# First feed-forward of a fused attention and two feed-forwards: six blocks of 512 tokens for eight of 384, and three weight slots shared by two tiles each

## The chip, the cores and the metric

One core of one Trainium2 chip runs the whole program. The metric is device time in microseconds; the kernel before takes 1082.54 us, the median of three runs (1082.47 to 1082.88).

## The reference

```python
# attention: 4 batch rows, 8 heads, 768 tokens, 64 wide; chunks of 32 tokens
# a chunk sees 16 tokens to its left, 8 to its right and 8 memory tokens
scores = (q_c @ k_full.transpose) / 8
a = softmax(scores); out[chunk] = a @ v_full
x = out as [3072 tokens, 512]
# first feed-forward: 512 -> 2048 -> 512
h = x @ w_in
g = where(h > 0, h, exp(min(h, 0)) - 1)
x = g @ w_out
# second feed-forward: 512 -> 1024 -> 1024 -> 512
a = x @ w1; b = x @ w2
out = ((a * b) @ w3) @ w_out2
```

The weights of both feed-forwards arrive as 64-bit floats and are decoded on the chip.

## The kernel before

Every value of a product is held as two tiles, a high part (`fp32r`) and a low part (the rest), and every product is three matmuls: high by high, high by low, low by high (`mm3`, L125 to L127 for the first feed-forward and the product of weights, L690 to L692 in `mm_half` for the second).

**Tiling.** Attention works on groups of 128 tokens (four chunks); 24 groups G, six to a batch row. The first feed-forward works on blocks of `TB` = 384 tokens, so three groups (`GPB`) make the input of a block, `xhl[j % 2]`. A block has 16 chunks f of 128 hidden features. For chunk n (counted over all blocks) `mm_h(n)` makes 12 matmuls into one of two PSUM banks, `elu_exp`, `elu_max`, `elu_hi`, `elu_lo` make g of it on ScalarE and VectorE, and `mm_x(n - 2)` makes 12 matmuls from an earlier chunk's g into four PSUM banks that gather over the block. `store_x1` writes a finished block to DRAM. The 32 weight tiles (16 of `w_in`, 16 of `w_out`) lie in slots `W[0]` to `W[31]`.

**Order of work.** The order on each engine is the one in which the code is written. Before the first matmul of block 0 stands `START`, a list of attention steps for the groups 0, 1, 2 (u and t: transposes of `head`, q and k; s: scores; m: max and exp; z, n, p: sums, normalising, 32x32 flip into `pT`; v: values; o: output split into `xhl`; k and w: loads) and steps f of the weight decoder `feed`. Groups 1 and 2 have PSUM pairs of their own; all other groups use `banks` (`PA`).

The attention of the later groups runs among the matmuls. Each chunk has two half-steps, called `at_step`: one behind `mm_h`, one behind `mm_x`. `base(G)` gives a group's first half-step, `paces["slow"]` the place of each of its steps behind that, with 32/3 half-steps from group to group. The same table places the decoding of the second feed-forward's weights: `wos` and `w3s` (a `w3` tile is turned by four TensorE transposes into `banks`, L442, and split into `st` by L173 and L176), and `duos` (differences of w1 and w2). At most two `st` tiles are live; a store to DRAM frees one.

In block 0 the decoder still works on `w_in` and `w_out`: per job a load of 512 KB, `rebase` (L160), `top` (L182) and a cast (L173) on ScalarE, `merge` (L186) or `shift` and `low` (L164, L168), and a split (L176) on VectorE.

Behind the blocks `mm_wc` multiplies the two last weight matrices (512 columns), and the second feed-forward takes four pairs of 384-token halves by seven products in place of eight.

Of the kernel before, what the change touches and what calls it, by code (L numbers as in the profile page):

```python
# [20 lines left out]
def tile_kernel(  # L21
# [24 lines left out]
    P = 128  # L46
# [13 lines left out]
    TB = 384  # L60
    NB = NT // TB
    GPB = TB // GQ
# [21 lines left out]
    W = [None if i in LATER else const.tile([P, 2, 512], F32R, name=f"w{i}") for i in range(2 * FF1)]  # L84
# [4 lines left out]
    PB = [pb_p.tile([P, 2, 512], F32, name=f"pair{i}") for i in range(GPB - 1)]  # L89
# [4 lines left out]
    x1d = [dram.tile([P, KT, TB], F32, name=f"x1d{j}") for j in range(NB)]  # L94

# [102 lines left out]
    class Feed:  # L198
# [19 lines left out]
        def step(self):  # L218
# [30 lines left out]
    def at_tile(G, pool, shape, name, tag=None):  # L249
        tag = tag or name  # L250
        if 0 < G < GPB:
            pool, tag = early_p, f"{tag}{G}"
        return pool.tile(shape, F32, tag=tag, name=name, bufs=1)
# [10 lines left out]
    def banks(G):  # L264
        return PB[G - 1] if 0 < G < GPB else PA

# [8 lines left out]
    def load_qk(G):  # L275
# [5 lines left out]
        kn_g = k_t[G] = at_tile(G, qk_p, [P, H, D], "kn") if 0 < G < GPB else kn  # L281
# [8 lines left out]
    def load_v(G):  # L290
# [5 lines left out]
        vw_g = v_t[G] = at_tile(G, v_p, [P, 2, H, D], "vw") if 0 < G < GPB else vw  # L296
        nc.sync.dma_start(out=vw_g[p0:P, 0], in_=by_token(v, b, t0 + p0, t0 + P))
        for c in range(NCG):
# [3 lines left out]
            if g == 0 or G < GPB:  # L302
# [187 lines left out]
    def store_next():  # L490
# [17 lines left out]
    def base(G):  # L508
        return 2 * FF1 * (G - GPB) // GPB + 1, "slow"
# [11 lines left out]
    def plan_duo(s0, duo):  # L521
        plan(s0, duo.jobs[0], (-1, rebase), (0.1, shift), (0.2, mid_low))
        plan(s0, duo.jobs[1], (1, rebase), (1.3, shift), (2.3, mid_low))
# [8 lines left out]
    DUOS = (1, 2, 4, 7, 10, 11, 13, 16)  # L532
    for G in range(GPB, NG):
        s0, pace = base(G)
        for at, fn in zip(paces[pace], chain):
# [3 lines left out]
        if G - GM in DUOS:  # L539
            plan_duo(s0, duos.pop(0))  # L540
        elif wos:
            plan(s0, wos.pop(0), (2, rebase), (3.5, shift), (4.5, mid_low), (5.1, mid_hi), (6.1, mid_lo))
        if w3s and G - GM not in (2, 11):
            plan(s0, w3s.pop(0), (5, rebase), (6.2, shift), (7.6, mid_low), (9.1, mid_flip), (9.6, mid_flip_lo))
# [106 lines left out]
    NPAIR = NB // 2  # L651
# [10 lines left out]
    def load_x1(p):  # L662
        for r in range(2):
            for k in range(2):
                t = late.tile([P, 2, TB], F32, tag=f"x1{r}{k}", name="x1")
                nc.sync.dma_start(out=t, in_=x1d[2 * p + r][:, 2 * k:2 * k + 2, :])
                x1_t[p, r, k] = t

    def left_step(p, i):
        a11, a12, a21, a22 = (x1_t[p, r, k] for r in range(2) for k in range(2))  # L670
        if i == 3:
            x1_t[p, "s1"] = sub(late.tile([P, 2, TB], F32, tag="s1", name="s1"), a21, a22, ALU.add)
        s1 = x1_t.get((p, "s1"))
        if i == 4:
            sub(a21, a11, a21)
            sub(a11, s1, a11)
        if i == 6:
            sub(a12, a12, a11)
        src = (a11, a12, a22, s1, a11, a21, a12)[i]
# [16 lines left out]

    def mm_step(n, last, between, stored):

        y, z = PS[4][:, 0:TB], PS[5][:, 0:TB]
# [15 lines left out]
        nc.scalar.copy(r1, y)  # L715
        mm_half(n, z, "a12", "b21", True, True)
        sub(c11, z, r1, ALU.add)
        do(0)
        mm_half(n, y, "s2", "t2", False, True)
        nc.scalar.copy(r2, y)  # L720
        do(1)
        mm_half(n, z, "s1", "t1", True, True)
        nc.scalar.copy(r5, z)
        do(2)
        mm_half(n, y, "s3", "t3", False, True)
        sub(c22, y, r5, ALU.add)
        do(3)
        mm_half(n, z, "s4", "b22", False, True)
        sub(c12, z, r2, ALU.add)
# [3 lines left out]
        sub(c22, y, c22, ALU.mult)  # L733
# [218 lines left out]
```

## Time and profile before

| | |
|---|---|
| median of three runs | 1082.54 us |
| profiled execution | 1081.98 us |
| its span, first to last instruction | 1080.2 us |
| TensorE matmul busy | 1044.0 us (97%) |
| VectorE busy | 573.2 us (53%) |
| ScalarE busy | 468.6 us (43%) |
| start, up to the first matmul of block 0 | 36.8 us |
| block 0 | 85.0 us |
| blocks 1 to 6 | 468.7 us |
| block 7 | 68.6 us |
| product of weights | 45.3 us |
| second feed-forward | 375.8 us |

A block is counted from its first matmul out of `xhl` to that of the next. Matmuls are pipelined and their ends are modelled, so the time that one matmul costs is read from start to start, not from its duration.

### The profile page before, as it was taken

The page shows a single profiled execution, that of the slowest core. Times are in us where ns is not written, and L with a number is a line of the kernel's source. Part 1 is how long each engine was busy: PE and PEld are TensorE (multiplying, and loading weights), DVE is VectorE, ACT ScalarE, POOL GpSimd, SP SyncE. Part 2 cuts the span into 40 slices and gives each one's busy share as a digit, 9 for nine tenths or more (in the row PEclk, how much of TensorE's full clock was granted, in tenths as well). Part 3 has the DMA queues.
Part 4 walks back from the last instruction along what each step waited for, and adds up shares of the span by engine and source line. Part 5 has one row for each costly group of instructions (what it writes and reads, how often), then busy time and mean ns, then how long its engine had stood idle before and what let it go on. Part 6 is the DMA issues. An engine that isn't in the chain of part 4 may idle for free.

```text
span 1080.2 us, 20847 instructions
## 1 busy us (share of the span) xinstructions
PE 1044.0 (97%) x8528; PEld 987.5 (91%) x8528; DVE 573.2 (53%) x1061; ACT 468.6 (43%) x984; POOL 1.7 (0%) x16
## 2 busy tenths in 40 slices
PE   4799999999999999999999999999999999999998
PEld 3788999999999999999999998799999999999997
DVE  4899667566565566566564334143443544443323
ACT  3788555555455555555554442032232222222222
POOL 0000000000000000000000000000000000000000
PEclk9999999999999999999999999999999999999999
DMA  8967356455455456454351865354565565555521
GB/s 192 292 177 212 107 174 184 132 166 155 131 161 174 143 158 183 147 169 142 100 163 44 296 215 172 131 181 143 172 217 208 169 217 208 171 167 188 182 78 59
DMA packets 170090, 180.40 MB, mean 167 GB/s; under 512 B 101388, under 2 KB 140300, under 8 KB 169996
## 3 DMA queue, kind: packets, MB, share of 16 engines
q1 hardware_dynamic: 168956, 178.81, 53.7%
q8 instruction: 67, 1.10, 0.4%
q10 hardware_dynamic: 1040, 0.26, 0.1%
q14 instruction: 27, 0.22, 0.1%
HBM read 139.20 MB, written 39.85 MB: 166 GB/s over the span
## 4 chain that ended last, share of the span: by engine, by line
PE 86%; DVE 6%; ACT 5%; issue 1%; DMA 1%; SPq 0%; ACTq 0%; DVEq 0%
PE bank L125 18%; PE bank L126 18%; PE bank L127 18%; PE bank L691 7%; PE bank L692 7%; PE bank L690 7%; PE banks L407 2%; PE banks L127 2%; PE banks L126 2%; PE banks L125 2%; PE banks L348 1%; PE banks L324 1%; DVE w L176 1%; DVE eg L574 1%; PE banks L326 1%
## 5 line engine op out<-in xcount | busy, mean ns | idle before, releaser
L125 PE MATMUL bank<-xhl,w 128*128 128x384 f32 x512 | 176.3, 344 | 0.7 <-ACT xhl L121 0.7
L125 PE MATMUL bank<-g,w 128*128 128x384 f32 x512 | 175.2, 342 | 0.0
L126 PE MATMUL bank<-g,w 128*128 128x384 f32 x512 | 171.4, 335 | 1.1 <-DVE g L582 1.1
L126 PE MATMUL bank<-xhl,w 128*128 128x384 f32 x512 | 171.9, 336 | 0.0
L127 PE MATMUL bank<-xhl,w 128*128 128x384 f32 x512 | 171.9, 336 | 0.0
L127 PE MATMUL bank<-g,w 128*128 128x384 f32 x512 | 171.3, 335 | 0.0
L578 ACT CAST g<-eg 128x384 fp32r<-128x384 f32 x128 | 66.0, 516 | 98.4 <-DVE eg L574 98.0
L574 DVE SCALAR_TENSOR_TENSOR eg<-eg,bank 128x384 f32<-128x384 f32 x128 | 70.2, 548 | 59.6 <-ACT eg L569 59.6
L125 PEld LDWEIGHTS bank<-xhl,w 128*128 128x128 f32 x512 | 96.6, 189 | 3.6 <-ACT xhl L121 0.9
L568 ACT ACTIVATE eg<-bank 128x384 f32<-128x384 f32 x128 | 62.8, 490 | 84.0 <-PE bank L127 83.9
L474 DVE TENSOR_TENSOR e<-bank,e 128x384 f32<-128x384 f32 x64 | 35.7, 558 | 118.9 <-PE bank L692 72.8
L126 PEld LDWEIGHTS bank<-g,w 128*128 128x128 f32 x512 | 96.2, 188 | 1.8 <-DVE g L582 1.8
L125 PEld LDWEIGHTS bank<-g,w 128*128 128x128 f32 x512 | 96.1, 188 | 1.1
L126 PEld LDWEIGHTS bank<-xhl,w 128*128 128x128 f32 x512 | 96.7, 189 | 0.4 <-DVE xhl L122 0.4
L127 PEld LDWEIGHTS bank<-xhl,w 128*128 128x128 f32 x512 | 96.5, 189 | 0.0
L127 PEld LDWEIGHTS bank<-g,w 128*128 128x128 f32 x512 | 96.1, 188 | 0.0
L738 ACT CAST g<-e 128x384 fp32r<-128x384 f32 x64 | 29.7, 512 | 145.9 <-DVE e L474 145.9
L582 DVE TENSOR_TENSOR g<-eg,g 128x384 fp32r<-128x384 f32 x128 | 70.6, 552 | 18.3 <-ACT g L578 18.3
L691 PE MATMUL bank<-xd,w 128*128 128x384 f32 x224 | 75.8, 338 | 0.0
L692 PE MATMUL bank<-xd,w 128*128 128x384 f32 x224 | 75.6, 337 | 0.0
L690 PE MATMUL bank<-xd,w 128*128 128x384 f32 x224 | 74.9, 334 | 0.0
L569 ACT ACTIVATE eg<-eg 128x384 f32<-128x384 f32 x128 | 67.3, 526 | 4.1
(145 smaller groups left out, 1829.6 us busy)
## 6 DMA issues: line engine op xcount, KB each, us to landing
w<-wqd SPq DMA_DIRECT2D x96, 512.0 KB
raw<-in_moe_w_dram SPq DMA_DIRECT2D x32, 512.0 KB
wqd<-st SPq DMA_DIRECT2D x24, 512.0 KB
raw<-in_moe_w_out_dram SPq DMA_DIRECT2D x20, 512.0 KB
w3d<-st SPq DMA_DIRECT2D x16, 512.0 KB
w<-w3d SPq DMA_DIRECT2D x16, 512.0 KB
w<-wqd SPq DMA_DIRECT2D x32, 256.0 KB
raw<-in_moe_w_in_dram SPq DMA_DIRECT2D x12, 512.0 KB
```

The costliest lines, as they stand in the source:

```text
L125: mm(o, lhsT=w_hi, rhs=x_hi, start=start, stop=False)
L126: mm(o, lhsT=w_hi, rhs=x_lo, start=False, stop=False)
L127: mm(o, lhsT=w_lo, rhs=x_hi, start=False, stop=stop)
L474: nc.vector.tensor_tensor(out=o, in0=a, in1=b, op=op)
L568: nc.scalar.activation(e, h_t[n], AF.Relu, scale=-1.0)
L569: nc.scalar.activation(e, e, AF.Exp, scale=-1.0)
L574: nc.vector.scalar_tensor_tensor(out=e, in0=e, scalar=-1.0, in1=h_t.pop(n), op0=ALU.add, op1=ALU.max)
L578: nc.scalar.copy(g_t[n][:, 0, :], eg_t[n])
L582: nc.vector.tensor_tensor(out=g[:, 1, :], in0=eg_t.pop(n), in1=g[:, 0, :].bitcast(F32), op=ALU.subtract)
L690: mm(o, lhsT=args[0], rhs=args[2], start=start and i == 0, stop=False, skip_group_check=more)
L691: mm(o, lhsT=args[0], rhs=args[3], start=False, stop=False, skip_group_check=more)
L692: mm(o, lhsT=args[1], rhs=args[2], start=False, stop=i == 1, skip_group_check=more)
```

## The change

The first feed-forward takes blocks of 512 tokens, so four groups make a block, there are six blocks, and a matmul has 512 columns. The second feed-forward keeps 384 (`TP`, `GPP`); it fetches its input from the 512-token blocks in up to two pieces.

`START` makes group 3 as well, with the q and k tiles, PSUM banks and `vw` of group 0, and has six decoder steps for five. The number of early PSUM pairs stays at two (`EARLY`).

The larger tiles need room. Slots 2, 3 and 4 hold the `w_out` tiles 24, 25 and 26 too: both are saved to DRAM (`shd`) after they were decoded, and in each block the slot is loaded with the one when the other was read (`fill`). The spare load buffers of the decoder fall from four to two; two tiles of the second feed-forward lie in other tiles' free columns, and `s1` is made in place.

A group gets 8 half-steps, with one pace for all. The `w3` turn moves from the half-step 9 of a group to 5, the values from 8 to 7, the output to 7.2, the first transposes of a batch row (`at_first`) to -0.5. Each odd group takes a `duo` and a `w3` tile, each even one a `wo` and a `w3` tile.

```diff
-    TB = 384
+    TB, TP = 512, 384
     NB = NT // TB
-    GPB = TB // GQ
+    GPB, GPP = TB // GQ, TP // GQ
+    EARLY = 3
...
-    RAWS, SPARE, SPARE_JOBS = 4, 4, 16
-    LATER = (10, 11, 12, 13, 14, 15, 25, 26, 27, 28, 29, 30, 31)
-    START = "u0 t0 f s0 t1 f m0 s1 z0 n0 m1 p0 t2 v0 s2 z1 n1 p1 m2 o0 k3 w3 v1 z2 n2 p2 f o1 v2 f o2 f"
+    RAWS, SPARE, SPARE_JOBS = 4, 2, 16
+    LATER = (11, 12, 13, 14, 15, 27, 28, 29, 30, 31)
+    SHARED = {2: 24, 3: 25, 4: 26}
+    START = "u0 t0 k3 f s0 t1 f m0 s1 z0 n0 m1 p0 t2 v0 w3 s2 z1 n1 p1 m2 o0 t3 v1 s3 z2 n2 p2 f o1 v2 m3 f o2 z3 n3 p3 k4 v3 w4 f o3 f"
...
+    for i, j in SHARED.items():
+        W[j] = W[i]
...
+            if 0 <= i - 3 < len(self.jobs) and self.jobs[i - 3].slot in shd:
+                slot = self.jobs[i - 3].slot
+                nc.sync.dma_start(out=shd[slot], in_=W[slot].bitcast(F32))
...
     def banks(G):
-        return PB[G - 1] if 0 < G < GPB else PA
+        return PB[G - 1] if 0 < G < EARLY else PA
...
-    paces = {
-        "slow": (-1, 0, 0, 2, 3, 4, 5, 6, 8, 8, 9), "fast": (-0.5, 0, 0, 1, 1.5, 2, 2.5, 3, 4, 4, 4.5),
-        "mid": (-1, 0, 0, 2, 3, 4, 5, 5, 7, 7, 7.5),
-    }
+    pace = (-0.5, 0, 0, 2, 3, 4, 5, 6, 7, 7.2, 7.5)
...
     def base(G):
-        return 2 * FF1 * (G - GPB) // GPB + 1, "slow"
+        return 2 * FF1 * (G - GPB) // GPB
...
-            (4.5, lambda d: d.hi(3, d.block(1, 1))), (5.1, Duo.lo),
-            (6.8, duo_first), (6.9, lambda d: d.hi(1)), (7.5, Duo.lo),
-            (10.3, duo_second), (10.4, lambda d: d.hi(2)), (11.1, Duo.lo),
+            (3.2, lambda d: d.hi(3, d.block(1, 1))), (4.2, Duo.lo),
+            (7.5, duo_first), (7.6, lambda d: d.hi(1)), (8.1, Duo.lo),
+            (8.2, duo_second), (8.3, lambda d: d.hi(2)), (9.1, Duo.lo),
...
+    def plan_w3(s0, at):
+        plan(s0, w3s.pop(0), (at, rebase), (max(at + 0.7, 3.6), shift), (4.2, mid_low), (5.1, mid_flip), (6.1, mid_flip_lo))
...
+            for a, b in SHARED.items():
+                if 1 <= j < NB and f == a + 1:
+                    fill(b, shd[b])
+                if j < NB - 1 and f == b - FF1 + 3:
+                    fill(a, shd[a])
```

Three places show how the order moves. In the changed kernel L122 has become L128, L176 is L182, L186 is L192, L317 is L326, L328 is L337, L365 and L366 are L374 and L375, L407 is L416, and L568 and L569 are L582 and L583.

VectorE at the start, behind the flip of group 2 (out of `e_538` before, `e_586` now); `pair_100`, `pair_101` and `banks` are the PSUM of the groups 1, 2 and 0 or 3. Before:

```order
L186 SCALAR_TENSOR_TENSOR f<-f,raw 128x512
L122 TENSOR_TENSOR xhl_73<-pair_100,xhl_73 128x2x4x64
L176 TENSOR_TENSOR w_75<-f,w_75 128x512
L186 SCALAR_TENSOR_TENSOR f<-f,raw 128x512
L122 TENSOR_TENSOR xhl_73<-pair_101,xhl_73 128x2x4x64
L176 TENSOR_TENSOR w_76<-f,w_76 128x512
L186 SCALAR_TENSOR_TENSOR f<-f,raw 128x512
L176 TENSOR_TENSOR w_77<-f,w_77 128x512
```

Now, with the passes of group 3 (L374, L375 and L382 on) between the output splits and the weights:

```order
L192 SCALAR_TENSOR_TENSOR f<-f,raw 128x512
L128 TENSOR_TENSOR xhl_73<-pair_100,xhl_73 128x2x4x64
L374 TENSOR_REDUCE mx<-banks 128x8
L375 TENSOR_TENSOR e<-banks,mx 128x512
L182 TENSOR_TENSOR w_75<-f,w_75 128x512
L192 SCALAR_TENSOR_TENSOR f<-f,raw 128x512
L128 TENSOR_TENSOR xhl_73<-pair_101,xhl_73 128x2x4x64
L382 TENSOR_REDUCE sm<-e 128x8
L383 TENSOR_SCALAR sm<-sm 128x8
L384 RECIPROCAL sm<-sm 128x8
L385 TENSOR_TENSOR rc<-sm,odd 128x16
L394 TENSOR_TENSOR e_653<-e,rc 128x16x32 x2
```

Group 3's max and subtract moved in ahead of the first weight's split, its sums and normalising ahead of the second's.

ScalarE in chunk 0 of block 0: the exponent of that chunk (`eg`, out of `bank_95`) and the copies of the first interleaved group's q and k (`qT`, `kT`). Before, the exponent comes first:

```order
L568 ACTIVATE eg<-bank_95 128x384
L569 ACTIVATE eg<-eg 128x384
L173 CAST w_78<-f 128x512
L160 ACTIVATE f<-more 128x512
L328 COPY qT<-banks 128x512
L331 COPY kT<-banks 128x16x32
L332 COPY kT<-banks 128x4x3x24
L333 COPY kT<-front 128x4x24
```

Now the six copies stand ahead of it:

```order
L179 CAST w_78<-f 128x512
L166 ACTIVATE f<-raw 128x512
L337 COPY qT<-banks 128x512
L340 COPY kT<-banks 128x16x32
L341 COPY kT<-banks 128x4x3x24
L342 COPY kT<-front 128x4x24
L343 COPY kT<-memo 128x16x8
L345 COPY front<-banks 128x96
L582 ACTIVATE eg<-bank_95 128x512
L583 ACTIVATE eg<-eg 128x512
```

The copies moved from behind the exponent and two decoder passes of the next weight to ahead of it, since the group's transposes stand one half-step earlier.

TensorE where a batch row ends (block 0, group 5 and the `head` of group 6): `pT,vw` are the values. Before, two sets of 12 matmuls lie between the values and the `head` transposes:

```order
L127 MATMUL bank_96<-xhl_73,w_1113 128x384
L407 MATMUL banks<-pT,vw 64x64 x32
L125 MATMUL bank_606<-g,w_1118 128x384
...
L127 MATMUL bank_609<-g,w_1119 128x384
L317 MATMUL banks<-ident,head 128x16 x4
L125 MATMUL bank_95<-xhl_74,w_75 128x384
```

Now nothing lies between them, and the next chunk's matmuls stand behind:

```order
L132 MATMUL bank_724<-g,w_91 128x512
L133 MATMUL bank_724<-g,w_91 128x512
L416 MATMUL banks<-pT,vw 64x64 x32
L326 MATMUL banks<-ident,head 128x16 x4
L131 MATMUL bank_95<-xhl_73,w_83 128x512
L132 MATMUL bank_95<-xhl_73,w_83 128x512
```

The `head` transposes moved up to the values of the group before, which use the same banks.

## Rows read from the trace of the kernel before

**Rows 1.** Page, part 1: engine, busy us (share of the span) x instructions.

```profile
PE 1044.0 (97%) x8528; PEld 987.5 (91%) x8528; DVE 573.2 (53%) x1061; ACT 468.6 (43%) x984; POOL 1.7 (0%) x16
```

**Rows 2.** Windows: from:to length, busy us of each engine, clock, DMA share, GB/s.

```profile
36.80:121.80 85.00, 78.08 (x785) 73.99 (x785) 74.53 (x136) 70.11 (x143) 0.00 (x0) 1.00 0.68 187
121.80:590.50 468.70, 466.54 (x4826) 451.24 (x4825) 287.53 (x566) 248.35 (x544) 0.00 (x0) 1.00 0.50 149
```

**Rows 3.** Timeline of TensorE, last block: start us, us, what; ends are modelled.

```profile
590.50 0.33 PE L125 MATMUL bank<-xhl,w 128*128 128x384 f32 x1
...
659.14 0.39 PE L125 MATMUL bank<-w,w 128*128 128x512 f32 x1
```

**Rows 4.** Timeline, weight product, 512 columns: first and last of 26 matmuls.

```profile
661.90 0.39 PE L125 MATMUL bank<-w,w 128*128 128x512 f32 x1
...
667.57 0.39 PE L126 MATMUL bank<-w,w 128*128 128x512 f32 x1
```

**Rows 5.** Timeline, all engines, start of the program; [idle before <-what ended it].

```profile
17.23 1.11 PE L324 MATMUL pair<-ident,qn 128*128 128x128 f32 x4
...
22.45 0.57 ACT L328 COPY qT<-pair 128x512 f32<-128x512 f32 x1
...
24.06 0.26 ACT L336 COPY front<-pair 128x96 f32<-128x96 f32 x1
...
25.29 1.25 SPq L141 DMA_DIRECT2D more<-in_moe_w_in_dram  x1
...
26.70 0.65 DVE L365 TENSOR_REDUCE mx<-pair 128x8 f32<-128x512 f32 x1
...
29.34 0.69 DVE L122 TENSOR_TENSOR xhl<-banks,xhl 128x512 fp32r<-128x512 f32 x1 [1.25 <-ACT xhl L121]
...
32.63 1.25 DVE L396 STREAM_TRANSPOSE pT<-e 128x1024 f32<-128x1024 f32 x1
...
33.80 0.65 DVE L186 SCALAR_TENSOR_TENSOR f<-f,raw 128x512 int32<-128x512 int32 x1
...
33.94 2.22 PE L407 MATMUL pair<-pT,vw 64*64 64x64 f32 x64 [4.88 <-DVE pT L396]
...
34.37 0.68 DVE L122 TENSOR_TENSOR xhl<-pair,xhl 128x512 fp32r<-128x512 f32 x1
...
34.48 0.62 ACT L173 CAST w<-f 128x512 fp32r<-128x512 f32 x1 [3.08 <-DVE f L186]
...
36.20 0.59 ACT L121 CAST xhl<-pair 128x512 fp32r<-128x512 f32 x1
...
36.83 0.69 PE L125 MATMUL bank<-xhl,w 128*128 128x384 f32 x1 [0.68 <-ACT xhl L121]
```

**Rows 6.** Timeline of TensorE, first block.

```profile
38.05 0.52 PE L127 MATMUL bank<-xhl,w 128*128 128x384 f32 x1
...
40.29 0.50 PE L125 MATMUL bank<-xhl,w 128*128 128x384 f32 x1
...
61.88 1.28 PE L407 MATMUL banks<-pT,vw 64*64 64x64 f32 x64 [1.84 <-DVE pT L396]
```

**Rows 7.** Timeline, values and output split of one group, sixth block.

```profile
455.07 1.16 PE L407 MATMUL banks<-pT,vw 64*64 64x64 f32 x64
...
456.16 0.45 PE L125 MATMUL bank<-xhl,w 128*128 128x384 f32 x1
...
456.94 0.69 DVE L122 TENSOR_TENSOR xhl<-banks,xhl 128x512 fp32r<-128x512 f32 x1 [2.82 <-ACT xhl L121]
```

**Rows 8.** Timeline of TensorE, fourth block: weight flip; wait ahead of the q transposes.

```profile
302.10 0.60 PE L442 MATMUL banks<-ident,f 128*128 128x128 f32 x4
302.45 0.42 PE L125 MATMUL bank<-g,w 128*128 128x384 f32 x1
...
304.45 0.34 PE L127 MATMUL bank<-g,w 128*128 128x384 f32 x1
305.15 0.65 PE L324 MATMUL banks<-ident,qn 128*128 128x128 f32 x4 [0.36 <-DVE st L176]
```

More of the change, by code (lines that the diff above doesn't have):

```diff
@@ L88, in tile_kernel @@
     pb_p = early_psum.enter_context(tc.tile_pool(name="pb_p", bufs=1, space=PSUM))
-    PB = [pb_p.tile([P, 2, 512], F32, name=f"pair{i}") for i in range(GPB - 1)]
+    PB = [pb_p.tile([P, 2, 512], F32, name=f"pair{i}") for i in range(EARLY - 1)]
     w3d = [[dram.tile([P, 2, 512], F32, name=f"w3d{h}_{c}") for c in range(FF2)] for h in range(2)]
@@ L94, in tile_kernel @@
     x1d = [dram.tile([P, KT, TB], F32, name=f"x1d{j}") for j in range(NB)]
+    shd = {i: dram.tile([P, 2, 512], F32, name=f"shd{i}") for pair in SHARED.items() for i in pair}
     early_ctx, w_ctx = ExitStack(), ctx.enter_context(ExitStack())
@@ L538, in tile_kernel @@
             continue
-        if G - GM in DUOS:
+        if G % 2:
             plan_duo(s0, duos.pop(0))
[L541 to L544, printed above, removed]
+            plan_w3(s0, 2.6)
+        elif G % GPB:
+            plan_wo(s0, 1)
+            plan_w3(s0, 2.6)
+        else:
+            plan_w3(s0, 3.4)
+            plan_wo(s0, 5.1)
     assert not wos and not w3s and not duos, (len(wos), len(w3s), len(duos))
@@ L732, in mm_step @@
         do(5)
-        sub(c22, y, c22, ALU.mult)
+        sub(c22, cut(y), c22, ALU.mult)
         sub(c11, c11, c12, ALU.mult)
@@ L805, in tile_kernel @@
                 late = ctx.enter_context(tc.tile_pool(name="late", bufs=1, side="right"))
-                more = [late.tile([P, 2, 2, TB], F32R, name=f"xc{i}") for i in range(3)]
+                more = [late.tile([P, 2, 2, TP], F32R, name=f"xc{i}") for i in range(3)]
                 left.append({})
                 for i, what in enumerate(LEFTS[:4]):
-                    left[0][what] = [xhl[i // 2][:, r, i % 2 * 2:i % 2 * 2 + 2, :] for r in range(2)]
+                    left[0][what] = [xhl[i // 2][:, r, i % 2 * 2:i % 2 * 2 + 2, 0:TP] for r in range(2)]
                 for i, what in enumerate(LEFTS[4:]):
@@ L860, in tile_kernel @@
             if n >= NH - FF1:
-                free = [f] if n < NH else []
+                free = [f] if n < NH and f not in SHARED else []
                 if n >= NH - FF1 + 2:
@@ L898, in tile_kernel @@
         end = ctx.enter_context(tc.tile_pool(name="end", bufs=1))
-        more = [end.tile([P, 2, 2, TB], F32R, name=f"xd{i}") for i in range(len(LEFTS))]
-        left.append({what: [t[:, r] for r in range(2)] for what, t in zip(LEFTS, more)})
-        e_f.update(enumerate([eg_p.tile([P, TB], F32, tag="eg", name="eg") for _ in range(2)] + [end.tile([P, TB], F32, name=f"e{i}") for i in range(4)]))
-        gq.extend([g_p.tile([P, 2, TB], F32R, tag="g", name="g") for _ in range(3)] + [end.tile([P, 2, TB], F32R, name="g3")])
+        gs = [g_p.tile([P, 2, TB], F32R, tag="g", name="g")[:, :, 0:TP] for _ in range(3)]
+        more = [end.tile([P, 2, 2, TP], F32R, name=f"xd{i}") for i in range(len(LEFTS) - 1)]
+        more = [[t[:, r] for r in range(2)] for t in more] + [[gs.pop(), end.tile([P, 2, TP], F32R, name="xd")]]
+        left.append(dict(zip(LEFTS, more)))
+        es = [eg_p.tile([P, TB], F32, tag="eg", name="eg")[:, 0:TP] for _ in range(2)]
+        es += [end.tile([P, TP], F32, name=f"e{i}") for i in range(4)]
+        e_f.update(enumerate(cut(e) for e in es))
+        gq.extend([[cut(g[:, i, :]) for i in range(2)] for g in gs])
+        gq.extend([[x[:, i, 0:GPP, TP:TB] for i in range(2)] for x in xhl])
         NA = NPAIR * FF2
@@ L915, in stored @@
                     store_out(p - 1, t)
-            mm_step(n, n == NA, {t: lambda t=t: behind(t) for t in range(2 * GPB)}, stored)
+            mm_step(n, n == NA, {t: lambda t=t: behind(t) for t in range(2 * GPP)}, stored)
             if n < NA:
```

68 lines of the change are left out of this document (38 added, 30 removed).

## The prediction

> **What bounds the kernel now.** I read the page's busy shares first: TensorE is busy for 97% of the span [rows 1]. So a change is worth what it takes off TensorE's own stream, or what it adds to the time in which TensorE waits. I then cut the span at the stage borders [rows 2]. The first block of the first feed-forward lasts 85.0 us, of which TensorE is busy for 78.1; in the same stretch VectorE is busy for 74.5 and ScalarE for 70.1, because the weights are decoded there. The next six blocks last 468.7 us with TensorE idle for only 2.2. The last block has no attention in it and the stages behind it are full as well. Outside the first 122 us the matmul stream therefore sets the pace.
>
> In the stream I took the distance from start to start, since the busy time of one matmul (0.33 us) overlaps with the next. The last block is 396 matmuls of 384 columns in 659.14 - 590.50 = 68.64 us, 173.3 ns each [rows 3]. The same three-term product with 512 columns stands in the stage that multiplies the two weight matrices: 25 matmuls in 667.57 - 661.90 = 5.67 us, 226.8 ns each [rows 4]. The difference is 53.5 ns for 128 columns; at 2.4 GHz 128 columns take 53.3. So each matmul has a fixed 13 ns that doesn't depend on its columns, and that is what the wider block saves.
>
> **The change, part by part.**
>
> *Wider matmuls.* 3072 matmuls of 384 columns become 2304 of 512, the same columns. 3072 x 173.3 = 532.4 us become 2304 x 226.8 = 522.5 us: **-9.9 us**, all of it on the path. The bound on the good side is this value. On the other side, the first twelve 512-column matmuls behind the switch of stage take 661.90 - 659.14 = 2.76 us, 230 ns each [rows 3, 4]; at that price the gain is 2.5. I take 226.8, because the feed-forward is a long run of one shape, as the 25 are.
>
> *A fourth group before the first matmul.* 512 tokens need four groups. Group 3 is the first that has no PSUM pair of its own: it reuses `banks`, so its transposes wait for group 0's output split, done at 29.34 + 0.69 = 30.0 [rows 5], and for its k, which is now issued right behind the load at 25.29. I put its transposes at 31.0 to 33.0 (two sets, 1.11 for the first [rows 5]). From there I follow the order of the changed kernel with the durations of [rows 5]. ScalarE: six copies 1.9 (22.45 to 24.32), to 34.9; then weight cast, rebase and top, which took 36.20 - 34.48 = 1.7, to 36.6; output cast of group 1, to 37.2. VectorE, which had been free at 34.4, waits for it: split 0.6, then group 3's max and subtract at 0.7 each, to 39.2. ScalarE: exp to 39.8, the next weight 1.7, output cast of group 2, to 42.1. VectorE: split to 42.7; sums, normalising and the 32x32 flip 3.9 (from 29.94, behind the split at 29.34, to 33.88), to 46.6. TensorE: values 2.2, to 48.9; output cast, to **49.5**. The first matmul stood at 36.83, so this costs **+12.7 us**. Its lower bound is +5.9, VectorE's own passes for one group (1.4 + 0.6 + 3.9) with nothing waiting; the upper one is +15, if k lands 2 us later. I stay with the walk.
>
> *One group less inside the blocks.* Six blocks with 18 groups take 468.7 us [rows 2]. Less 2304 x 173.3 ns = 399.3, less six waits of 0.53 (305.15 - 304.45 less one distance), less 16 weight flips of 0.35 (302.10 to 302.45) [rows 8], 60.6 us are left, 3.4 for a group. 21 groups were interleaved, now 20: **-3.4 us**.
>
> *The new pace.* A group has eight half-steps of 2.7 us and more where it had 10.67 of 2.1. The weight flip moves from just ahead of the next group's transposes to the half-step before the values, with VectorE's pass a whole matmul set ahead of them. So the six waits on `st` go: **-3.2 us** [rows 8]. From the values to the next transposes there remain one matmul set of 2.7 us and the output split. That takes 456.94 + 0.69 - 456.16 = 1.5 us after the values [rows 7], and is covered; without the cover it would cost these 1.5 us for each group. Once a batch row ends, the cover is gone: for groups 6, 12 and 18 the four `head` transposes now stand directly behind the values of the group before (half-step -0.5, that is 7.5 of that group, behind 7.2), in the same banks. TensorE waits 1.5 us there, three times, with the matmuls of the block queued behind it: **+4.4 us**. It can't be less than the two passes; in the first block it can be 1 us more.
>
> *The first block.* Before, TensorE idled 6.9 us in it [rows 2]; the largest wait shown is 1.84 us for the flip `pT` at 61.88 [rows 6]. Now group 4's copies stand ahead of the first chunk's relu on ScalarE, and its values stand four matmul sets behind its scores. Counted from the first matmul: product 4.5 (at the lower clock, below), transposes 1.0, copies 1.9, relu and exp 1.3, so VectorE starts the first max at +8.8. Up to the end of the flip it has 26 passes: fifteen of 0.60 (33.80 to 34.37 is the nearest pair [rows 5]), the rest of the attention and two shifts, 16.1 together, to +24.9. TensorE is at the values at 4.5 + 1.0 + 2.7 + 0.8 + 4 x 2.7 = +19.9. It waits **5.0 us**. For groups 5 to 7 the max starts as soon as the exp allows, and by the same count the flip ends about when TensorE arrives; I add 0.3 for all three, bound 0 to 6. With 0.7 at the start, 1.0 for the clock, it is 7.0 against 6.9: **+0.1 us**.
>
> *The clock.* The first matmuls stand 0.32 us apart from 38.05 to 40.29, which is 384 columns at 1.2 GHz, after TensorE had mostly waited [rows 6]. Ten of 512 columns at that level cost more than ten of 384: **+0.5 us**. After the new wait of 5.0 us the lower level can come back: the values took 2.2 at it and 1.1 at the full clock [rows 5, 7], and some matmuls may follow. I priced it at 1.0 above; the bounds are 0 and 3. The Trainium skill (TensorE: Matmul & The Clock Gate, Part 1) says that an idle TensorE falls back to half its clock; no wait in the blocks before is long enough to show it.
>
> *Shared slots, x1 in pieces, the later stages.* Three slots are loaded twice a block, 512 KB each: 30 more loads over 500 us. Each is issued one chunk after the slot's last reader and needed seven chunks later, about 38 us, behind a DMA load of 0.50 in these blocks [rows 2]. I cost it at nothing; uncovered, one would cost its transfer, some 3 us. The second feed-forward keeps 384 tokens and its instructions. 0.
>
> **Sum.** -9.9 + 12.7 - 3.4 - 3.2 + 4.4 + 0.1 + 0.5 = **+1.2 us**, against the profiled execution of 1081.98 us (span 1080.2). The median of the runs is 0.56 above that, so 1082.54 + 1.2 = **1083.7 us**. What the wider matmuls give, the start takes.
>
> **Rivals.**
>
> *The start is shorter, faster.* If VectorE doesn't wait for ScalarE's copies, the fourth group costs nearer its 5.9 us. For it speaks that VectorE is the busiest engine there; against it, the order of the changed kernel puts copies and weight casts ahead of the output cast that VectorE waits for. Midway (9) and with half the 5.0 us wait: 1083.7 - 3.7 - 2.5 = 1077.5.
>
> *The first block runs on VectorE, slower.* Decoding, the wider ELU and four groups are about 24 us of VectorE for each 25.5 us of TensorE. If the flip of groups 5 to 7 comes 1.5 us late each, and the clock stays low after the long wait (2 more), it is 1083.7 + 4.2 + 2 = 1090. It decides from a flip that ends behind TensorE's arrival; my count leaves it under 1 us.
>
> *The cost grows with the columns, slower.* If the 13 ns were a share of the columns, a 512-column matmul would take 173.3 x 4/3 = 231 ns and the gain would be gone: 1083.7 + 9.7 = 1093. The 25 matmuls at 226.8 speak against it [rows 4]. The Trainium skill (TensorE: Matmul & The Clock Gate, Back-to-back issue gap) gives columns / 2.4 + 2.5 ns, 162.5 and 215.8 here; by it the gain would be 1.9 us and the time 1092. Both of its values are below the rows, so I give it little.
>
> *The change isn't what it says.* A shared slot comes late and TensorE waits for it: two slots by five blocks at 1 us is +10, 1094. TensorE idles 2.2 us in six blocks before, which are the six waits on `st` [rows 2, 8], none on a DMA, and the lead is 38 us.
>
> **How the numbers follow.** A measurement of this kernel can tell about 0.2% (2.2 us) from no change, so faster is below 1080.4 and slower above 1084.7. My forecast has 0.55, its own range is 1079.5 to 1087.5: 0.09 faster, 0.31 same, 0.15 slower. The shorter start has 0.24, of which 0.20 is faster and 0.04 same. The slower first block has 0.13, the column cost 0.05, the late slot 0.03, all slower except 0.01. Together 0.29 faster, 0.36 same, 0.35 slower. The range has to reach the first two rivals: 1076.0 to 1090.0 leaves out the last two and the ends of the others, about 0.2.
>
> **What would show it.** First matmul of the feed-forward at 48 to 51 us; starts 227 ns apart in the blocks; a wait of about 5 us for `pT` at the first values in the first block; three waits of 1.5 us before the `head` transposes; no wait for `st` at the transposes of q; the second block starting near 159; the last feed-forward matmul again near 660. If the first matmul comes at 45 or the 5 us wait is missing, I am wrong to the fast side; if waits for `pT` or for DMA stand in the later blocks, to the slow side.

## The result, and the profile after

The changed kernel takes 1090.11 us, the median of six runs (1089.22 to 1092.42), against 1082.51 for the kernel before: a ratio of 1.0073, with a 95% interval of 1.0060 to 1.0086. It is slower by 0.7%, where "no change" was forecast, and 0.1 us outside the range. The profiled execution took 1091.64 us with a span of 1089.9, against 1081.98 and 1080.2 before, so profile to profile the difference is 9.7 us.

The page's first part and the same cut by stages as before [rows 1, 2] (from:to, length, then busy us of PE, PEld, DVE, ACT and POOL, the granted clock, the DMA share and GB/s):

```profile
PE 1039.5 (95%) x7760; PEld 888.9 (82%) x7760; DVE 569.1 (52%) x993; ACT 456.6 (42%) x884; POOL 1.7 (0%) x16
```

```profile
51.30:161.00 109.70, 103.69 (x927) 84.07 (x928) 83.18 (x145) 77.58 (x150) 0.00 (x0) 0.96 0.68 195
161.00:577.80 416.80, 411.12 (x3780) 333.90 (x3779) 260.28 (x473) 217.99 (x425) 0.00 (x0) 1.00 0.62 190
```

TensorE is still the engine that is nearly always busy. But its idle time between the first block and the last was 2.2 us in 468.7 before; now it is 5.7 in 416.8. The timeline of TensorE at the start of the program, in the first block, in the middle of block 3 (the fourth; blocks count from 0), and behind the last block (start, duration, in brackets the idle time before and what ended it):

```profile
33.01 1.09 PE L333 MATMUL banks<-ident,qn 128*128 128x128 f32 x4 [7.03 <-DMA qn<-in_q_dram]
...
48.57 2.01 PE L416 MATMUL banks<-pT,vw 64*64 64x64 f32 x64 [6.58 <-DVE pT L405]
51.29 0.79 PE L131 MATMUL bank<-xhl,w 128*128 128x512 f32 x1 [0.70 <-ACT xhl L127]
...
52.60 0.63 PE L133 MATMUL bank<-xhl,w 128*128 128x512 f32 x1
...
56.44 0.63 PE L133 MATMUL bank<-xhl,w 128*128 128x512 f32 x1
56.87 0.98 PE L333 MATMUL banks<-ident,qn 128*128 128x128 f32 x4
57.69 0.60 PE L335 MATMUL banks<-ident,kn 128*128 128x128 f32 x4
...
77.61 1.82 PE L416 MATMUL banks<-pT,vw 64*64 64x64 f32 x64 [4.25 <-DVE pT L405]
79.36 0.79 PE L131 MATMUL bank<-xhl,w 128*128 128x512 f32 x1
...
416.14 1.16 PE L416 MATMUL banks<-pT,vw 64*64 64x64 f32 x64
418.76 0.42 PE L326 MATMUL banks<-ident,head 16*128 16x16 f32 x4 [1.46 <-DVE xhl L128]
...
420.25 0.63 PE L131 MATMUL bank<-xhl,w 128*128 128x512 f32 x1
420.68 0.63 PE L132 MATMUL bank<-xhl,w 128*128 128x512 f32 x1
...
668.67 0.39 PE L131 MATMUL bank<-w,w 128*128 128x512 f32 x1
```

The first feed-forward matmul stands at 51.29 us (36.83 before [rows 5]), the weight product begins at 668.67 (659.14 before [rows 3]). So the start takes 14.5 us more, the first feed-forward 4.9 less, and the stages behind it are the same: 1089.9 - 668.7 = 421.2 us against 1080.2 - 659.1 = 421.1. Blocks two to six have a new entry in TensorE's table of waits (total us, times, longest):

```profile
PE bank L132 <- DVE g L596: 3.6, 5, 0.8
PE banks L326 <- DVE xhl L128: 2.9, 2, 1.5
```

L596 makes the low part of `g`, the elu's output. In the kernel before, TensorE waited for it only in the first block. Here is one of the five places, the start of the third block, on ScalarE, VectorE and TensorE:

```profile
267.52 0.65 ACT L179 CAST st<-st 128x512 fp32r<-128x512 f32 x1
```

```profile
268.20 0.69 DVE L182 TENSOR_TENSOR st<-st 128x512 fp32r<-128x512 f32 x1 [3.46 <-ACT st L179]
268.81 0.68 DVE L596 TENSOR_TENSOR g<-eg,g 128x512 fp32r<-128x512 f32 x1
```

```profile
268.32 0.39 PE L131 MATMUL bank<-g,w 128*128 128x512 f32 x1
269.55 0.50 PE L132 MATMUL bank<-g,w 128*128 128x512 f32 x1 [0.84 <-DVE g L596]
```

VectorE had nothing to do for 3.46 us: it stood at a pass for the later stages' weights (`st`), the low part of a `duo`'s third tile, whose cast comes on ScalarE behind the six copies of the group's qT and kT. The low part of `g`, due at once, stands behind that pass. TensorE's matmuls on `g` are 1.23 us apart there, and not 0.227.

At the start of the third block of the kernel before, the same two passes stand in the same order on VectorE. But the cast stood ahead of the copies on ScalarE, and the low part of `g` was over 1.6 us before TensorE's first matmul on `g` (202.40):

```profile
198.95 0.62 ACT L173 CAST st<-st 128x512 fp32r<-128x512 f32 x1 [0.74 <-DVE st L474]
...
202.76 0.57 ACT L328 COPY qT<-banks 128x512 f32<-128x512 f32 x1
```

```profile
199.60 0.69 DVE L176 TENSOR_TENSOR st<-st 128x512 fp32r<-128x512 f32 x1 [0.69 <-ACT st L173]
200.21 0.55 DVE L582 TENSOR_TENSOR g<-eg,g 128x384 fp32r<-128x384 f32 x1
```

The transposes of a block's first group now stand a half-step earlier (the `+ 1` that left `base`), and so their copies have come ahead of that cast.

To see where the 4.9 us of the first feed-forward come from, I took every distance from one matmul's start to the next in both traces and sorted them. In microseconds:

| part of the first feed-forward | before | after | difference |
|---|---|---|---|
| 3071 x 173.3 ns, 2303 x 226.8 ns | 532.2 | 522.3 | -9.9 |
| inserts (attention, weight flips) with the waits ahead of them | 77.0 | 74.6 | -2.4 |
| waits inside the matmul sets (over 250 ns each) | 2.3 | 5.6 | +3.3 |
| the rest: clock at half, first matmuls behind an insert | 10.6 | 14.6 | +4.0 |
| from the first to the last matmul | 622.1 | 617.2 | -5.0 |

In the last row but one, matmuls at the lower clock make up 4.1 us of the 14.6 (21 distances of 382 to 428 ns, nearly all 427).

### The profile page after: what moved, and what is told of

Same layout as the page of the kernel before. It is cut to its first block, busy times and chain, and to the rows that moved or that the text cites. A ratio compares the mean times of both kernels' runs of the same rounds, so it can differ in the third digit from the quotient of the medians.

```text
span 1089.9 us, 19197 instructions
## 1 busy us (share of the span) xinstructions
PE 1039.5 (95%) x7760; PEld 888.9 (82%) x7760; DVE 569.1 (52%) x993; ACT 456.6 (42%) x884; POOL 1.7 (0%) x16
## 4 chain that ended last, share of the span: by engine, by line
PE 91%; ACT 3%; DVE 2%; DMA 2%; SPq 1%; issue 0%; ACTq 0%; DVEq 0%
PE bank L131 20%; PE bank L132 19%; PE bank L133 19%; PE bank L710 7%; PE bank L711 7%; PE bank L709 7%; PE banks L416 2%; PE banks L133 2%; PE banks L132 2%; PE banks L131 2%; PE banks L357 1%; PE banks L333 1%; PE banks L335 1%; DMA vw<-in_v_dram 1%; PE banks L451 1%; DMA qn<-in_q_dram 1%
## 5 line engine op out<-in xcount | busy, mean ns | idle before, releaser
L131 PE MATMUL bank<-xhl,w 128*128 128x512 f32 x384 | 156.2, 407 | 1.0 <-ACT xhl L127 0.7
L132 PE MATMUL bank<-g,w 128*128 128x512 f32 x384 | 150.6, 392 | 3.6 <-DVE g L596 3.6
L131 PE MATMUL bank<-g,w 128*128 128x512 f32 x384 | 153.2, 399 | 0.0
L132 PE MATMUL bank<-xhl,w 128*128 128x512 f32 x384 | 152.0, 396 | 0.0
L133 PE MATMUL bank<-xhl,w 128*128 128x512 f32 x384 | 152.0, 396 | 0.0
L133 PE MATMUL bank<-g,w 128*128 128x512 f32 x384 | 150.1, 391 | 0.0
L582 ACT ACTIVATE eg<-bank 128x512 f32<-128x512 f32 x96 | 57.3, 597 | 121.2 <-PE bank L133 121.1
L588 DVE SCALAR_TENSOR_TENSOR eg<-eg,bank 128x512 f32<-128x512 f32 x96 | 65.6, 683 | 75.9 <-ACT eg L583 75.7
L132 PEld LDWEIGHTS bank<-g,w 128*128 128x128 f32 x384 | 72.2, 188 | 19.5 <-DVE g L596 5.6
L131 PEld LDWEIGHTS bank<-xhl,w 128*128 128x128 f32 x384 | 73.3, 191 | 16.7 <-ACT xhl L127 0.9
L133 PEld LDWEIGHTS bank<-xhl,w 128*128 128x128 f32 x384 | 73.4, 191 | 15.9
L132 PEld LDWEIGHTS bank<-xhl,w 128*128 128x128 f32 x384 | 73.4, 191 | 14.8 <-DVE xhl L128 0.4
L131 PEld LDWEIGHTS bank<-g,w 128*128 128x128 f32 x384 | 72.2, 188 | 15.8 <-ACT g L592 0.2
L133 PEld LDWEIGHTS bank<-g,w 128*128 128x128 f32 x384 | 72.1, 188 | 15.1
L592 ACT CAST g<-eg 128x512 fp32r<-128x512 f32 x96 | 59.6, 621 | 35.4 <-DVE eg L588 35.1
L596 DVE TENSOR_TENSOR g<-eg,g 128x512 fp32r<-128x512 f32 x96 | 65.7, 684 | 14.8 <-ACT g L592 14.5
L483 DVE TENSOR_TENSOR e<-bank,eg 128x384 f32<-128x384 f32 x64 | 35.6, 557 | 58.8 <-PE bank L711 58.8
L583 ACT ACTIVATE eg<-eg 128x512 f32<-128x512 f32 x96 | 60.7, 632 | 3.1
```

The lines of the kernel that those rows point to most:

```text
L131: mm(o, lhsT=w_hi, rhs=x_hi, start=start, stop=False)
L132: mm(o, lhsT=w_hi, rhs=x_lo, start=False, stop=False)
L133: mm(o, lhsT=w_lo, rhs=x_hi, start=False, stop=stop)
L483: nc.vector.tensor_tensor(out=o, in0=a, in1=b, op=op)
L582: nc.scalar.activation(e, h_t[n], AF.Relu, scale=-1.0)
L583: nc.scalar.activation(e, e, AF.Exp, scale=-1.0)
```

## The experiments

All edits are to the changed kernel, and differences are between medians, against its 1090.11 us, unless another kernel is named. The kernel before took 1082.4 to 1082.6 beside each of them. My theory after the comparison was that four places lose time independently: the `head` transposes, the low part of `g` at a block's start, the load of the fourth group's q, and the elu work of the first chunk. The rivals were that a wait which is taken away comes back a step later, and that the shared slots' transfers are behind it.

**e1_head: the `head` transposes one step later.**

```
-        for at, fn in zip(pace, chain):
+        for at, fn in zip((0, 1, 1) + pace[3:] if G % GPS == 0 else pace, chain):
```

> Edit: the groups that begin a block (6, 12 and 18) take their three `head` transposes one step later, behind the first unit's output, as in the kernel before; nothing else changes. Theory A (the three waits of 1.5 us on the low part of x and the clock's fall to half behind the one at group 18 are costs of the new place in the order): the three gaps at L326 go, the low clock from 419 to 423 us goes, and the time falls by 3 x 1.5 + 1.7 = 6 us, to about 1084. Theory B (what waits there is due anyway, and waits one step later): the gaps move to L326 or L333 one step on, the time stays within 1 us of 1090.

The groups 6, 12 and 18 begin a batch row; of them only 12 begins a block. The edit moves their q and k transposes and the load behind these by a step too.

Measured: 1084.07 us (1082.57 to 1085.54), -6.0; ratio to the kernel before 1.0015 (1.0005 to 1.0024). No wait at L326 is left, and only this stands in TensorE's table of waits from 161 us on:

```profile
PE bank L132 <- DVE g L596: 2.7, 4, 0.8
```

The granted clock stays at 1.0 from 83 us to the end of the blocks. So the three `head` waits were pure cost, as theory A says, but that the gain meets the forecast to the tenth is luck. There were five waits for the low part of `g`, and the one of the third block is gone as well, which is another 1.0 us: group 12 begins that block, its copies now stand behind the cast, and the low part of `g` is over at 265.8, before TensorE's first matmul on `g` (266.03):

```profile
263.88 0.62 ACT L179 CAST st<-st 128x512 fp32r<-128x512 f32 x1 [1.14 <-DVE st L483]
...
266.61 0.56 ACT L337 COPY qT<-banks 128x512 f32<-128x512 f32 x1
```

```profile
265.15 0.68 DVE L596 TENSOR_TENSOR g<-eg,g 128x512 fp32r<-128x512 f32 x1
```

With the three waits and the fall of the clock that is 4.4 + 1.0 + 1.6 = 7.0 us. About 1 us came back, in part at the start (0.3 later in this execution) and behind the wait for `pT`, where eight matmuls run at the lower clock and not four.

**e2_glo: the low part of `g` ahead of the step's attention work, at the start of a block.**

```
+            early_lo = FF1 < n < NH and at == 0
+            if early_lo:
+                elu_lo(n - 1)
             at_step()
...
-            if FF1 < n < NH:
+            if FF1 < n < NH and not early_lo:
                 elu_lo(n - 1)
```

> Edit: where a block begins, the last low part of g of the block before (L596) is put on VectorE ahead of that step's attention work and not behind it; nothing else changes. Theory A (the five waits of PE on L596, at the start of each block from the second on, come from its place behind the low part that waits for ScalarE's cast): four gaps of about 1.2 us and one of 0.4 go, the time falls by 3.5 to 4 us, to about 1086.5. Theory B (the low part is late since ScalarE's elu work is late, whatever stands before it): PE still waits there, and the time stays within 1 us of 1090.

Measured: 1085.40 us (1083.95 to 1088.40), -4.7; ratio to the kernel before 1.0030 (1.0020 to 1.0040). The same place as above, VectorE and TensorE:

```profile
264.80 0.68 DVE L596 TENSOR_TENSOR g<-eg,g 128x512 fp32r<-128x512 f32 x1
268.34 0.69 DVE L182 TENSOR_TENSOR st<-st 128x512 fp32r<-128x512 f32 x1 [2.86 <-ACT st L179]
```

```profile
268.46 0.39 PE L131 MATMUL bank<-g,w 128*128 128x512 f32 x1
268.68 0.39 PE L132 MATMUL bank<-g,w 128*128 128x512 f32 x1
```

The low part is now done before VectorE turns to `st`, and the matmuls are 0.22 us apart. VectorE still waits for ScalarE's cast, but nobody waits for VectorE. Theory A: ScalarE wasn't late for the elu, only the order on VectorE was wrong. The gain is 0.7 above the expected range. In this kernel's profile the clock doesn't fall at 419 us either, although the wait at that `head` is still there; some 1.6 us in one execution come from that.

**e3_k3: the fourth group's q and k requested earlier.**

```
         load_v(1)
+        at_first(0)
+        at_turn(0)
+        load_qk(3)
         feed.load(3)
...
-    START = "u0 t0 k3 f s0 t1 ...
+    START = "f s0 t1 ...
```

> Edit: the q and k of the fourth group are requested right behind the first values and ahead of the weights of the first feed-forward's third pair; the rest of the start's order stays. Theory A (the 7.0 us in which the fourth group's transposes wait for their q set the first feed-forward matmul at 51.3 us): the wait at L333 falls to 2 us or less, the first feed-forward matmul comes near 48 us, the time falls by about 3 us to 1087. Theory B (behind the q the chain over VectorE is as late: split, maximum and low parts of the fourth group): the wait goes, the start does not move by more than 1 us, and neither does the time.

Measured: 1088.24 us (1087.78 to 1088.68), -1.9, and 3.6 from profile to profile; ratio to the kernel before 1.0052 (1.0037 to 1.0067). The start on TensorE:

```profile
29.62 1.11 PE L333 MATMUL banks<-ident,qn 128*128 128x128 f32 x4 [3.78 <-DVE xhl L128]
...
45.13 2.01 PE L416 MATMUL banks<-pT,vw 64*64 64x64 f32 x64 [7.50 <-DVE pT L405]
...
47.84 0.79 PE L131 MATMUL bank<-xhl,w 128*128 128x512 f32 x1 [0.71 <-ACT xhl L127]
```

The transposes start 3.4 us earlier and wait for the output split of group 0, as the prediction had it, no longer for the load. Their wait falls to 3.78 us, not to 2. All that follows moves by the same 3.4. Theory A, with a size that the medians put lower than the profiles. Some of that gap is the kernel it is compared with: the profiled execution of the changed kernel was 1.5 us above its median, and in the profiles of the kernels whose order at the start is the same the first matmul stands between 50.2 (e5_nofill) and 51.6 (e1_head).

**e4_exp: the first chunk's exponential ahead of group 4's copies.**

```
-            if n < NH and not spread:
+            if n < NH and (n == 0 or not spread):
                 elu_exp(n)
             at_step()
-            if spread:
+            if spread and n:
                 elu_exp(n)
```

> Edit: in the first block's first step ScalarE takes the exponential of the elu ahead of the copies of group 4, and not behind them. Theory A (VectorE is behind in the first block since its elu work comes late and then stands ahead of the copy of pT): the wait of 4.2 us on pT at the first values falls by about 2 us, and the low clock behind it shrinks; the time falls by 2 to 3 us. Theory B (VectorE's total of work ahead of that copy is the limit, whatever the order on ScalarE): the wait stays at 4 to 5 us, the time stays within 1 us of 1090.

Measured: 1089.07 us (1088.33 to 1090.03), -1.0; ratio to the kernel before 1.0060 (1.0045 to 1.0075). VectorE gets the elu at 57.94 us and not at 61.40, and then waits for ScalarE once more, at the next weight:

```profile
57.94 0.69 DVE L588 SCALAR_TENSOR_TENSOR eg<-eg,bank 128x512 f32<-128x512 f32 x1 [2.31 <-ACT eg L583]
60.23 0.69 DVE L182 TENSOR_TENSOR w<-f,w 128x512 fp32r<-128x512 f32 x1 [1.60 <-ACT w L179]
```

The values wait 3.86 us for `pT` (4.25 in the changed kernel). So it is theory B within a little: an earlier exponential moves ScalarE's other work behind it, and the wait shrinks by 0.4 us. The ranges of the two kernels overlap, so the size of the gain, 1.0, is uncertain.

**e5_nofill: the shared slots neither saved nor refilled.**

```
-                nc.sync.dma_start(out=shd[slot], in_=W[slot].bitcast(F32))
+                pass
...
-            for a, b in SHARED.items():
+            for a, b in ():
```

> Edit: the three shared slots are neither saved nor refilled, so that from the second pass on they hold whichever tile was there last; this leaves out 6 saves and the reloads of every block, and the output is computed with wrong weights in those places. All instructions on the engines stay. Theory A (the slots' transfers lie beside work: no wait of PE on a transfer stands in the blocks of the changed kernel): the time stays within 1 us of 1090.1. Theory B (the added 0.5 MB tiles slow the queues that the attention's loads and the weights of the later stages share, so that others come late): the time falls by 2 us or more, and a wait on a transfer or a raised pitch goes with it.

Measured: 1090.80 us (1088.48 to 1091.47), +0.7 and within its own spread; ratio to the kernel before 1.0073 (1.0058 to 1.0088). Theory A: the slots cost nothing that shows, as forecast.

**e6_all: the edits of e1_head, e2_glo, e3_k3 and e4_exp together.**

> Edit: the edits of e1_head, e2_glo, e3_k3 and e4_exp together. Theory A (four separate losses at four places): the gains add, 6.0 + 4.7 + 1.9 + 1.0 = 13.6 us, the time is about 1076.5 and the kernel beats the one before by 6 us. Theory B (they share a part, the fall of the clock behind a wait, which e1_head and e2_glo both lost): 1.7 us is counted twice, the time is about 1078.2.

Measured: 1076.48 us (1075.98 to 1076.84), -13.6; ratio to the kernel before 0.9944 (0.9929 to 0.9959). The six blocks now beat the eight. That the four gains add to the tenth, as theory A has it, is luck: e1_head and e2_glo hold two things in common, the wait of the third block (1.0 us) and, in their profiles, the fall of the clock (1.6). Between profiled executions the four gains are 6.1, 6.1, 3.6 and 1.6 us, 17.4 together, and e6_all has 14.9, which is 2.5 less. The medians don't show this overlap; whether a fall of the clock is in every execution the runs don't tell. The first feed-forward takes 605.6 us from its first to its last matmul (622.1 before), and its first matmul stands at 47.9.

**e7_late: group 4's values one slot later, behind 12 more matmuls (from e6_all).**

```
+        first_pace = pace[:8] + (8, 8.2, 8.5) if G == GPB else (0.5, 1, 1) + pace[3:] if G == GPB + 1 else pace
-        for at, fn in zip((0, 1, 1) + pace[3:] if G % GPS == 0 else pace, chain):
+        for at, fn in zip((0, 1, 1) + pace[3:] if G % GPS == 0 else first_pace, chain):
```

> Edit: e6_all, with the values and the output of group 4 one slot later, behind 12 more matmuls of the feed-forward (2.7 us), and the transposes of group 5 one slot later, behind that output; the rest stays. Theory A (VectorE is behind in the first block at that one place, by 4 to 5 us, and catches up later): the wait for pT falls by 2.7 us to about 1.5 us, the low clock behind it (6.8 us at half in e1_head) shrinks or goes, and the time falls by 2.7 to 5 us against e6_all. Theory B (VectorE bounds the whole first block): the wait moves to the scores or values of group 5, or to the elu work, and the time stays within 1 us of e6_all.

Measured: 1073.08 us (1072.65 to 1073.87), -3.4 against e6_all; ratio to the kernel before 0.9915 (0.9898 to 0.9931). The values, and the transposes of group 5 behind them:

```profile
72.27 1.28 PE L416 MATMUL banks<-pT,vw 64*64 64x64 f32 x64 [1.13 <-DVE pT L405]
77.47 0.66 PE L333 MATMUL banks<-ident,qn 128*128 128x128 f32 x4 [0.97 <-DVE xhl L128]
```

The wait for `pT` falls to 1.13 us, the clock stays at 1.0 behind it, and a smaller wait of 0.97 appears at group 5's transposes. Theory A: the wait falls by 2.64 us for 2.7 us of matmuls (3.77 in e6_all), so VectorE isn't the bound of the whole block. The new wait of 0.97 at group 5 is of the kind that theory B expected, but small.

**e8_warm: 14 unread matmuls while TensorE waits for the fourth group's `pT` (from e6_all).**

```
+            if what == "v2":
+                for _ in range(14):
+                    mm(PS[5], lhsT=W[0][:, 0, 0:P], rhs=W[0][:, 0, :], start=True, stop=True)
```

> Edit: e6_all, with 14 matmuls of 512 columns that nobody reads put on PE behind the third group's values, where PE waits 7.5 us for the fourth group's pT; they write a bank that the first feed-forward fills later from new. Theory A (the granted clock falls to half in that wait, and some 10 matmuls of the first feed-forward run at 427 ns and not 227 before it rises): the clock stands at 1.0 by the first feed-forward matmul, and the time falls by about 2 us against e6_all. Theory B (the low clock lies where VectorE sets the pace in the first block anyway, so what PE gains there it waits again for pT at the first values): the matmuls run at 227 ns from the start, the wait for pT grows by as much, the time stays within 0.7 us of e6_all.

Measured: 1074.71 us (1073.94 to 1074.94), -1.8 against e6_all; ratio to the kernel before 0.9927 (0.9912 to 0.9942).

```profile
37.84 5.04 PE L820 MATMUL bank<-w 128*128 128x512 f32 x14
45.00 1.28 PE L416 MATMUL banks<-pT,vw 64*64 64x64 f32 x64 [2.11 <-DVE pT L405]
46.95 0.50 PE L131 MATMUL bank<-xhl,w 128*128 128x512 f32 x1 [0.68 <-ACT xhl L127]
...
69.84 2.01 PE L416 MATMUL banks<-pT,vw 64*64 64x64 f32 x64 [3.79 <-DVE pT L405]
```

The clock stands at 1.0 from 41 us, the values take 1.28 us (2.01 in the changed kernel), and the feed-forward starts 1.0 us earlier than in e6_all. The wait for `pT` in the block stays at 3.8 and doesn't grow. Theory A: in this kernel the low clock at the start is worth 1.8 us.

**e9_best: e7_late with the 14 matmuls.**

> Edit: e7_late with the 14 unread matmuls of e8_warm. Theory A (the low clock at the start and the wait for pT are separate losses): the gains of 3.4 and 1.8 us against e6_all (1076.5) add, the time is about 1071.3. Theory B (in e8_warm the higher clock let VectorE's work catch up less than the matmuls, and now PE waits again for pT or for the output of group 4): the wait for pT grows back by what the clock gives, and the time stays at 1072.5 to 1073.5.

Measured: 1072.46 us (1071.69 to 1073.52); ratio to the kernel before 0.9908 (0.9894 to 0.9922). Against e7_late that is -0.6, with ranges that overlap: the gains don't add, as theory B says, but not for its reason.

```profile
38.83 3.47 PE L821 MATMUL bank<-w 128*128 128x512 f32 x14
45.48 1.28 PE L416 MATMUL banks<-pT,vw 64*64 64x64 f32 x64 [3.18 <-DVE pT L405]
47.44 0.80 PE L131 MATMUL bank<-xhl,w 128*128 128x512 f32 x1 [0.68 <-ACT xhl L127]
48.16 0.79 PE L132 MATMUL bank<-xhl,w 128*128 128x512 f32 x1
```

In this execution, the slowest of the four, the 14 matmuls ran at the full clock, took 3.47 us and not 5.04, and were over at 42.3 us. TensorE then waited 3.18 us, and the clock fell just as the feed-forward began. Filler that is counted in matmuls covers less time when the clock is up. In the profile of e10_turn below, with the same filler, it took 4.69 us, TensorE waited 1.26 us behind it, and the clock stayed up.

**e10_turn: group 5's transposes, scores and maximum one slot later (from e9_best).**

```
- ... (0.5, 1, 1) + pace[3:] if G == GPB + 1 ...
+ ... (0.5, 2, 2, 3, 4, 5, 5.5) + pace[7:] if G == GPB + 1 ...
```

> Edit: e9_best, with the transposes of group 5 one more slot later and its scores and maximum one slot later too, so that the output of group 4 is written before they come. Theory A (the wait of 1.35 us at the transposes of group 5 in e7_late is a place in the order like those at the heads): it goes, and the time falls by 1 us against e9_best. Theory B (VectorE has no slack there, so that the later maximum makes pT of group 5 late): a wait of 1 us or more stands at the values of group 5, and the time is within 0.5 us of e9_best, or above it.

Measured: 1074.59 us (1072.39 to 1075.60), 2.1 above e9_best; ratio to the kernel before 0.9928 (0.9914 to 0.9941). The wait at the transposes is gone, and stands at the values of group 5:

```profile
94.43 1.28 PE L416 MATMUL banks<-pT,vw 64*64 64x64 f32 x64 [1.64 <-DVE pT L405]
```

Theory B: for group 5 VectorE has less slack than the step by which its maximum was moved. A wait of 0.97 us (in e7_late; the 1.35 above is the distance from the matmul before) was traded for one of 1.64. That is 0.7 of the 2.1 us. The profiled execution, 1072.39 us, is the fastest of the five, so what makes the others slower isn't in this trace.

## Why the prediction was wrong

The forecast said that the start takes what the wider matmuls give. The two large terms came out nearly so. What tipped it were losses behind the first block that the sum had at nothing.

*Wider matmuls: right.* The settled distance is 226 to 227 ns, and the table's first row has the -9.9 us. The rival in which the cost grows with the columns is out; so is the value of 215.8 ns by the formula of the Trainium skill (TensorE: Matmul & The Clock Gate, Back-to-back issue gap), which that section gives for an isolated matmul, and by which the gain would have been 1.9. A small part was given back: behind an insert the second to the sixth distance are 229 to 236 ns before they settle, which with the first one makes 1.1 us more than before over the whole stage (the last row but one of the table, +4.0, less the clock's share there, 4.1 - 1.2). At 384 columns they were within a few nanoseconds of 173 from the second on. I didn't test why.

*The start: right in kind, 1.8 us short.* The walk put group 3's transposes at 31.0, released by group 0's output split. They came at 33.01, released by the load of q, which stands behind a weight's load in the queue:

```profile
25.99 0.90 SPq L147 DMA_DIRECT2D more<-in_moe_w_in_dram  x1
27.00 0.43 SPq L296 DMA_DIRECT2D qn<-in_q_dram  x1
```

The prediction named the load of k as the upper bound ("if k lands 2 us later") and took the value without it. e3_k3 shows the walk's own releaser once the load is earlier.

*One group less, and the new pace: right in size.* The inserts became 2.4 us shorter; -3.4 - 3.2 + 4.4 is -2.2. No wait for `st` stands ahead of the q transposes, and the three `head` waits measure 1.46 us each. e1_head takes them away, 3 x 1.46 = 4.4.

*The step that failed: the waits that the new pace brings.* For the blocks behind the first one, the term for the new pace takes six waits on `st` away (-3.2) and adds the `head` waits (+4.4). Any other wait there stood at nothing, without a look at VectorE's order where a block begins. The six waits did go; they hung on the split of a turned `w3` tile. But the new pace also took the transposes a half-step earlier and so put six copies ahead of a `duo`'s cast on ScalarE, VectorE's pass waits for that cast, and the low part of `g` stands behind the pass, where TensorE needs it at once. That is 1.0 us at four block starts (1.23 less 0.23 from start to start), 4.0 us that the sum didn't have. In the second block no `duo` is under way; there the copies stand ahead of the cast of `g` itself, 0.4 us, which stays in e2_glo. Two edits take such waits away: e2_glo puts the low part of `g` ahead of the pass, and e1_head, at the third block, puts the copies behind the cast. At the fourth and fifth block the order is the same as at the third, in the sixth it isn't: no group follows, and the cast waits for the `duo`'s sums, which stand in that half-step as well.

The blocks from the second on took 668.7 - 161.0 = 507.6 us, and the prediction had 660.3 - 159 = 501.3, 6.3 less. The 4.4 us are most of that. The fall of the clock below, 1.6, and the slower first distances, 1.1, would make it 7.1; the prediction gave both borders as "near", so 0.8 us more or less say nothing.

*The first block: right, in part by luck.* It was to start at 49.5 and end near 159, 109.5 us; it took 109.7. Its wait for `pT` is 4.25 us (5.0 forecast), and the lower clock in it cost about 1 us more than the forecast, which all but cancel. The measured time equals that of the rival in which this block runs on VectorE, 1090, but its mechanism isn't there: no wait for `pT` stands at groups 5 to 7, and e7_late takes most of the one wait away by moving one group's values.

*The clock: too small.* I allowed 0.5 us for the start, 1.0 behind the wait for `pT`, nothing later. At the start ten matmuls are 427 ns apart (52.60 to 56.87), which is 10 x 0.2 = 2.0 us, and the q transposes behind them took 0.4 us longer than before; the kernel before lost some 1.2 at its smaller matmuls [rows 6]. So it is 1.2 more and not 0.5. Behind the wait for `pT` the values took 1.75 us to the next matmul, where 1.09 is usual [rows 7], and four matmuls lost 0.75: 1.4 together. Behind the `head` wait of block 3 eight more matmuls ran at the lower clock, 1.6 us. That a wait of 1.46 us would bring the clock down was in no term.

*The shared slots, the later stages: right*, 0 (e5_nofill, and 421.2 against 421.1 us).

In the sum: 1.8 at the start, 0.2 in the first block, 6.3 behind it and 0.1 in the later stages make 8.4 of the 8.5 us by which the profiled execution (1091.64) exceeds 1081.98 + 1.2. The median of the runs is 1.5 us lower than that execution. How much of that is the fall at 419 us, which need not be in every execution, and how much the start, stays open.

## What to carry to other kernels

A step that is moved earlier moves ahead of all that stood between its old place and its new one, on each engine that it uses. Here a group's transposes came a half-step earlier. Their six copies came to stand ahead of a cast on ScalarE, a pass on VectorE waited for the cast, and the next instruction in VectorE's queue, which had nothing to do with that group, made TensorE wait. So list for each engine what the moved step now stands ahead of, and follow each of these into the queue of the engine that reads it. Where a larger tile spaces the work out, go through every border (the start of the program, of a block, of a batch row) and ask for each engine which instruction is due first and which one stands first. Here four such places, worth 13.6 us together, decided between slower and faster, and a change of order was enough at each.

## What the hardware showed that was not expected

The granted clock fell to half, 1.2 GHz, behind waits of only 1.46 us. In the profiles of the five kernels that keep the three `head` waits (the changed one, e2_glo, e3_k3, e4_exp, e5_nofill) the clock fell shortly behind such a wait at 419 us; nowhere; at 260; at 261; at 106 and at 420 us. That is 5 of 15 waits, at about 1.6 us each, each kernel seen in one execution. In the six kernels without these waits (e1_head, e6_all, e7_late, e8_warm, e9_best, e10_turn) the clock never fell between 83 us and the end of the blocks. The length of the wait doesn't decide it: in the first block of the kernel before, waits of 1.84 [rows 6] and 1.82 us brought no fall. The `head` waits differ from those in what stands ahead of them, 64 small matmuls of the values (416.14 above) and not a set of the feed-forward. But the same wait did it in one place and not in another; what decides it I can't tell from these runs. The Trainium skill (TensorE: Matmul & The Clock Gate, Why this matters for your kernels) warns only of longer idle gaps; by that rule e1_head would have gained the 4.4 us of the three waits and the 1.0 of the third block at most, and it gained 6.0.
